# Copying negated scores to SBUF while their maximum is taken, in a planned attention-and-Fourier kernel

## The chip, the cores and the metric

The kernel runs on one core of a Trainium2 chip. Five engines work side by side, each through its own fixed list of instructions: TensorE (PE, with its weight loader PEld) multiplies matrices, VectorE (DVE), ScalarE (ACT) and GpSimd (POOL) work on tiles, and SyncE (SP) issues the transfers between HBM and SBUF. Engines wait for each other by semaphores. Matmuls write to PSUM, a small memory of banks of 512 float32 values per partition. The metric is the device time of one execution in microseconds. The kernel before takes 2978.28 us (median of 3 runs, 2978.08 to 2978.9).

## The reference

Two independent layers, their outputs side by side. All data are float32; S = 2048 rows, D = 1024 columns, 32 heads of 32 columns.

```python
qkv = x @ wqkv                       # 2048 x 1024 by 1024 x 3072, split in 32 heads
scores = q @ k.T * 32 ** -0.5        # per head: 2048 x 2048
p = softmax(scores, axis=-1)
a = (p @ v, heads joined) @ wo

re, im = xb @ dft_hid_re.T, xb @ dft_hid_im.T
b = dft_seq_re @ re - dft_seq_im @ im
out = concat([a, b], axis=-1)        # 2048 x 2048
```

The inputs of the attention half are scaled up by 8, so the scores spread widely and a softmax without its row maximum would overflow.

## The kernel before

**Dense products.** The products of the projections and of the Fourier layer are done by a seven-product scheme on 2 x 2 blocks (the products are numbered 1 to 7), and each product in three matmuls of a reduced-precision float type: every operand is split in a high part (a cast, line 475) and a low part (the difference, line 478), and high x high, low x high and high x low are summed in PSUM (line 389). Operands come by DMA, some after sums of two or three blocks (line 453), and results are combined out of PSUM by VectorE. In the planner these matmuls are the list `fills`, in one fixed order: the projections of x, then `dense1` and `dense2` of the Fourier layer, and last `project`, the output projection, whose operands need the result of attention.

**Attention, per head, twice over the scores.** `scores(h)` computes the 2048 x 2048 scores with queries on the partitions, in 32 tiles of 128 x 1024: two matmuls into a PSUM buffer of two banks (`psS`, two buffers, line 1193), a row maximum by VectorE, negated, into one column of `negm` (line 1199), and an exponential by ScalarE with that as its bias, which is wanted only for its row sum (`sums`, line 1202): the exponentials themselves are written back over the scores in PSUM and never read. From `negm` a per-row maximum is made, moved by DMA into two extra rows of the query operand, and `transposed(h)` then computes the same scores with keys on the partitions, maximum already subtracted, in 64 tiles of 128 x 512 (`psT`, two buffers, line 1316); ScalarE's exponential writes each into an SBUF tile `pt` or `ptl` (line 1320). Those tiles come from a ring of `NPT` = 27, five of them (`NLOW`) in another pool. After 5, 5 and 6 groups of four tiles (`ENDS`), a block of matmuls multiplies them with the values (line 1335) and gives the tiles back; VectorE adds the blocks up (lines 1346 and 1348).

**The order of work.** All engines' lists are written out ahead of time by a planner (`Plan`), a small simulation with a constant for each kind of operation (in us: `MAX` 1.22 for the row maximum, `ES` and `ET` for the two exponentials, `EVAC`, `CAST` and so on). A `Ring` stands for a set of buffers: `take()` gives the operations that must end before the next buffer is free. VectorE, ScalarE, GpSimd and SyncE take the ready operation of the lowest rank. TensorE chooses between three streams, S (score tiles), T (transposed tiles) and V (the blocks with the values), and the fills. An attention operation is taken only `LATE` = 0.25 us after its operands and buffers are free in the plan, as a reserve against the plan's errors. Scores may run ahead of the transposed tiles up to `LEAD`. A fill is taken when no stream is ready, or when the fills are behind their share of the work. The engines then keep the planned order at run time and wait where reality is later than the plan.

The first head's scores (h = 0) are computed while the first projection products still hold their buffers; heads 1 to 31 follow when the attention pools (`att()`, `att_low()`) have been opened.

Of the kernel before, what the change touches and what calls it, by code (L numbers as in the profile page):

```python
# [8 lines left out]
F32 = mybir.dt.float32  # L9
F32R = mybir.dt.float32r  # L10
AF = mybir.ActivationFunctionType
ALU = mybir.AluOpType
# [4 lines left out]
P = 128  # L17
S = 2048
# [3 lines left out]
NC = D // P  # L22
NS = S // P
NB = 512
NPT = 27
NE = 4
NLOW = 5
ENDS = (0, 5, 10, 16)
# [33 lines left out]
class Plan:  # L62
# [23 lines left out]
    def op(self, engine, cost, emit, after=(), uses=(), rank=0.0, kb=0, order=None, other=None, lanes=1, two=False):  # L86

        o = Op(engine, cost, emit, rank, kb, other, two)  # L90
        o.lanes = lanes
        seen = set()
        for d in after:
            if d is not None and id(d) not in seen:
                seen.add(id(d))
                self._wait(o, d)
        for u in uses:
            u.append(o)
        if order is not None:
            p, order.first = order.first, o  # L100
            if p is not None and not p.begun:
                p.soon.append(o)
                o.left += 1
        if o.left == 0:
            self._release(o)
        return o
# [104 lines left out]
def kernel(  # L211
# [11 lines left out]
    nc = tc.nc  # L223
# [26 lines left out]
    def f(ap):  # L250
        return ap.bitcast(F32)
# [74 lines left out]
    def att_low():  # L326

        att()
        return late["atl"]
# [6 lines left out]

    MM, PV, SWITCH, TINY = 0.2275, 0.853, 0.40, 0.17
    ES, ET = 1.235, 0.625
    MAX, EVAC, CAST, BIT = 1.22, 0.685, 0.415, 0.275
    SUB = 1.31  # L340
    ISSUE = 0.46

    LATE = 0.25
    HB = 0
    ACAST = 0.6
    RES = 400
# [11 lines left out]
    op = pl.op  # L358
# [798 lines left out]
    streams = {n: [] for n in "STV"}  # L1157
    psS_r, psT_r, pt_r, vt_r, rt_r, ot_r = Ring(2), Ring(2), Ring(NPT), Ring(2), Ring(1), Ring(2)
    small = {n: Ring(b) for n, b in (("st", 2), ("nm", 2), ("lh", 2), ("tw", 1))}
    qx_r = Ring(1)  # L1160
    got = {}
    Tops, Sops = {}, {}
    exp_of = {}
# [5 lines left out]
    def scores(h):  # L1169
        ST = {}  # L1170
        sold, suse = small["st"].take()
        maxes, exps = [], []
        if h:
            xold, xuse = qx_r.take()

            def load_x():
                att()
                g, r0 = divmod(h, 4)
                nc.sync.dma_start(f(QX[0])[0 : 3 * DH], qk_d[2 * g][0][r0 * DH : r0 * DH + DH].rearrange("d i c -> (d i) c"))

            got[h, "x"] = op("SP", ISSUE, load_x, [*xold, *qk_st[2 * (h // 4)][0], *(att_gate if h == 1 else [])], [xuse], -2, 192)
        for n, (qt, c) in enumerate([(k % 4, k // 4) for k in range(8)] + [divmod(k, 2) for k in range(8, 32)]):
            old, users = psS_r.take()
            own = h > 0 and qt < 4
            box = {}

            def mm(n=n, qt=qt, c=c, box=box, own=own):
                if n == 0:
                    ST["negm"] = sm.tile([P, 2, NS], F32, name="negm", bufs=2)
                    ST["sums"] = sm.tile([P, 2, NS], F32, name="sums", bufs=2)  # L1190
                box["p"] = p = psS.tile([P, 1024], F32, name="psS")
                for i in range(2):
                    nc.tensor.matmul(  # L1193
                        p[:, i * NB : i * NB + NB], (QX[0] if own else QS[h % 2])[:, qt * P : qt * P + P],
                        KS[h % 2][:, c * 1024 + i * NB : c * 1024 + i * NB + NB], start=True, stop=True,
                    )

            def mx(qt=qt, c=c, box=box):
                nc.vector.tensor_reduce(out=ST["negm"][:, c, qt : qt + 1], in_=box["p"], axis=AX.X, op=ALU.max, negate=True)  # L1199

            def ex(qt=qt, c=c, box=box):
                nc.scalar.activation(box["p"], box["p"], AF.Exp, bias=ST["negm"][:, c, qt : qt + 1], accum_out=ST["sums"][:, c, qt : qt + 1])  # L1202

            a = op("PE", 2 * MM, mm, [*old, *([got.get((h, "x"))] if own else [got.get((h, 0, qt // 4)), got.get((h, "z"))]), got.get((h, 1, 2 * c)), got.get((h, 1, 2 * c + 1))],
                   [users, xuse] if own else [users])
            b = op("DVE", MAX, mx, [a] + (sold if n == 0 else []), [users, suse], 0)
            e = op("ACT", ES, ex, [b], [users, suse], 0)
            exp_of[a] = e
            maxes.append(b)
            exps.append(e)  # L1210
            Sops.setdefault(h, []).append(a)
            streams["S"].append((a, h, n))
            if n == 5 and h:
                sums(h - 1)

        nold, nuse = small["nm"].take()
        lold, luse = small["lh"].take()
        box = {}

        def nmin():  # L1220
            ST["nm"] = sm.tile([P, NS], F32, name="nm", bufs=2)
            nc.vector.tensor_reduce(out=ST["nm"], in_=ST["negm"].rearrange("p c n -> p n c"), axis=AX.X, op=ALU.min)

        def high():
            box["l"] = sm.tile([P, 2, NS], F32R, name="lh", bufs=2)
            nc.vector.tensor_reduce(out=box["l"][:, 0], in_=ST["negm"].rearrange("p c n -> p n c"), axis=AX.X, op=ALU.min)

        def low():
            nc.vector.tensor_tensor(out=box["l"][:, 1], in0=ST["nm"], in1=f(box["l"])[:, 0], op=ALU.subtract)

        b = op("DVE", TINY, high, maxes + lold, [luse, suse], -2)
        a = op("DVE", TINY, nmin, maxes + nold, [nuse, suse], -2)
        c = op("DVE", TINY, low, [a, b], [nuse, luse], -2, two=True)
        def across():
            box["t"] = sm.tile([P, 2 * NS], F32, name="lt", bufs=2)
            nc.vector.transpose(box["t"], f(box["l"]).rearrange("p i s -> p (i s)"))

        d = op("DVE", TINY, across, [b, c], [luse], -2)

        put = op("SP", ISSUE, lambda: nc.sync.dma_start(m_d[h].rearrange("i (g p) -> g i p", g=4), box["t"]), [d], [luse], -3, 32)  # L1240
        moved = [op("SP", ISSUE, lambda: nc.sync.dma_start(f(QS[h % 2])[96:98, :], m_d[h].rearrange("(i q) p -> i (q p)", i=2)), [put], [], -3, 16)]
        mine[h] = (ST, suse, nuse, exps, moved)
# [59 lines left out]
    def transposed(h):  # L1302
# [4 lines left out]
        for t in range(NS):  # L1307
            for j in range(4):
                old, users = psT_r.take()
                here = pt_r.n % NPT < NLOW  # L1310
                pold, puse = pt_r.take()
# [6 lines left out]
                def ex(box=box, here=here):  # L1318
                    box["t"] = att_low().tile([P, NB], F32, name="ptl", bufs=NLOW) if here else att().tile([P, NB], F32, name="pt", bufs=NPT - NLOW)
                    nc.scalar.activation(box["t"], box["p"], AF.Exp)  # L1320
# [75 lines left out]
    while nf < len(fills) or any(place[n] < len(s) for n, s in streams.items()):  # L1396
# [18 lines left out]
        for n, (o, h, k) in heads.items():  # L1415
            if o.left:
                continue
            ready = o.ready + LATE
            if n == "V":
                ready = max(ready, room)  # L1420
            if ready > pl.now:
                times.append(ready)
                continue
            if n == "V":

                near = any(m in heads and heads[m][0].left == 0 and heads[m][0].ready + LATE < pl.now + NEAR and not (m == "S" and held) for m in "ST")
                if (near or stock < STOCK) and pl.now < o.ready + PATIENCE:
                    times.append(o.ready + PATIENCE)
                    continue
            rank = {"V": 0, "T": 1, "S": 0.5 if stock > SFIRST else 1.5}[n]  # L1430
            if n == "S" and "T" in heads and heads["T"][0].left == 0:
                th, tk = heads["T"][1:]
                lead = k / 33.0 * SST + 16 * (h - th - 1) - tk / 4
                if lead > LEAD:
                    continue
                if lead > 0:
                    rank = 2
            ok.append((rank, n))
        fill = None
        if nf < len(fills):  # L1440
            o, first, left = fills[nf]
            ready = o.ready if o.left == 0 else 1e18
            if first:
                ready = max(ready, room)
            if ready + (LATE if first else 0.0) <= pl.now:
                fill = o
            elif ready < 1e17:
                times.append(ready + LATE)
        if fill is not None and (not ok or (not first and left <= HB) or nf / (FILL - RES) <= done / ATT):
# [6 lines left out]
        if ok:  # L1456
            n = min(ok)[1]
            o = heads[n][0]
# [47 lines left out]
```

## Time and profile before

| What | Value |
|---|---|
| median of 3 runs | 2978.28 us (2978.08 to 2978.9) |
| profiled execution: span from its first to its last instruction | 2976.1 us |
| mean granted TensorE clock | 1.000 |
| busy: TensorE, weight loader | 99%, 72% |
| busy: VectorE, ScalarE, GpSimd | 81%, 77%, 29% |
| row maxima (line 1199) | 1024 of 1219 ns |
| exponentials of scores (line 1202), with a separate read of the sum | 1024 of 1143 ns, and 260 ns |
| exponentials of transposed tiles (line 1320) | 2048 of 654 ns |
| DMA | 58.6% of 16 engines' span, 188 GB/s |

Times are microseconds unless marked ns. An engine is busy while an instruction's record runs; records on one engine overlap a little, so a mean duration is longer than the distance from one start to the next. TensorE's matmuls are pipelined: one of 512 columns is on record for 390 ns, and the next starts long before that is over. The profile tells idle time before an instruction and what ended it ("<-").

### The profile page before, as it was taken

The numbers are of one execution on the slowest core, as the hardware profiler recorded it, in microseconds if no ns is written. First come the engines' busy times: TensorE is split into PE (matmuls) and PEld (weight loads), VectorE is DVE, ScalarE is ACT, GpSimd is POOL, SyncE is SP. The second block draws the span as 40 slices with busy tenths as digits, with TensorE's granted clock in tenths as the row PEclk, the third lists the DMA queues.
The fourth block names the chain that finished last, engine by engine and source line by source line (L and its number), as shares of the span: only waits on it lengthen the run. The fifth ranks groups of instructions, "written<-read, shape, count | busy, mean of one in ns | idle before, by whom it ended". The sixth has DMA issues, their size and how long they took to land. (4 is left out here: it accounts for less than half of the span.)

```text
span 2976.1 us, 45423 instructions
## 1 busy us (share of the span) xinstructions
PE 2950.9 (99%) x14912; PEld 2136.2 (72%) x14912; DVE 2403.6 (81%) x3237; ACT 2285.9 (77%) x4314; POOL 868.7 (29%) x641
## 2 busy tenths in 40 slices
PE   9999999999999999999999999999999999999999
PEld 7886766777777777777777667677777666677787
DVE  7678889788877877777778898888777888887696
ACT  5347888888888888888888888888888888887431
POOL 2312425122212332131102443332012534342152
PEclk9999999999999999999999999999999999999999
DMA  9974658666625655554425775555334775555662
GB/s 347 357 228 161 196 181 284 220 218 227 209 74 193 193 155 160 172 177 149 153 87 170 226 226 166 162 165 164 113 110 137 228 248 174 160 181 179 229 229 98
DMA packets 376576, 558.56 MB, mean 188 GB/s; under 512 B 111100, under 2 KB 111100, under 8 KB 376220
## 3 DMA queue, kind: packets, MB, share of 16 engines
q1 hardware_dynamic: 376344, 555.68, 58.6%
q8 instruction: 120, 1.97, 0.3%
q14 instruction: 112, 0.92, 0.1%
HBM read 402.42 MB, written 153.11 MB: 187 GB/s over the span
## 5 line engine op out<-in xcount | busy, mean ns | idle before, releaser
L1199 DVE TENSOR_REDUCE negm<-psS 128x1 f32<-128x1024 f32 x1024 | 1240.6, 1219 | 194.8 <-PE psS L1193 189.6
L1202 ACT ACTIVATE psS<-psS,negm 128x1024 f32<-128x1024 f32 x1024 | 1170.7, 1143 | 104.2 <-DVE negm L1199 99.2
L1320 ACT ACTIVATE pt<-psT 128x512 f32<-128x512 f32 x1668 | 964.9, 654 | 270.7 <-PE psT L1316 268.6
L389 PE MATMUL pd<-slot,h 128*128 128x512 f32 x3368 | 1145.7, 390 | 1.2 <-DVE ot L1346 0.9
L1316 PE MATMUL psT<-qs,ks 128*128 128x512 f32 x2048 | 804.9, 396 | 0.0
L389 PEld LDWEIGHTS pd<-slot,h 128*128 128x128 f32 x3368 | 632.3, 188 | 133.7 <-DVE h L475 1.3
L389 PE MATMUL pd<-slot,l 128*128 128x512 f32 x1684 | 656.4, 390 | 0.7 <-POOL l L478 0.7
L1316 PEld LDWEIGHTS psT<-qs,ks 128*128 128x128 f32 x2048 | 381.6, 188 | 169.5 <-issue 62.9
L1193 PE MATMUL psS<-ks,qs 128*128 128x512 f32 x1552 | 476.2, 392 | 7.1 <-ACT psS L1202 6.5
L478 POOL TENSOR_TENSOR l<-raw,h 128x512 fp32r<-128x512 f32 x160 | 214.6, 1341 | 828.9 <-PE psT L1316 344.8
L1335 PE MATMUL pd<-pt,vt 128*32 128x512 f32 x3336 | 430.6, 594 | 0.2
L453 POOL TENSOR_TENSOR raw<-raw,g 128x512 f32<-128x512 f32 x216 | 285.7, 1329 | 439.1 <-issue 74.8
L389 PEld LDWEIGHTS pd<-slot,l 128*128 128x128 f32 x1684 | 316.2, 188 | 67.4 <-POOL l L478 1.0
L1193 PEld LDWEIGHTS psS<-ks,qs 128*128 128x128 f32 x1552 | 288.5, 188 | 76.4 <-ACT psS L1202 17.9
L478 POOL TENSOR_TENSOR slot<-raw,slot 128x512 fp32r<-128x512 f32 x143 | 206.6, 1453 | 432.9 <-DVE slot L475 203.1
L1335 PEld LDWEIGHTS pd<-pt,vt 128*32 128x32 f32 x3336 | 111.3, 110 | 230.2 <-issue 216.4
L1320 ACT ACTIVATE ptl<-psT 128x512 f32<-128x512 f32 x380 | 224.5, 654 | 59.9 <-PE psT L1316 59.5
L1202 ACT ACTIVATION_READ_ACCUMULATOR psS<-psS,negm 128x1 f32 x1024 | 266.6, 260 | 0.0
L389 PE MATMUL pd<-slot,slot 128*128 128x512 f32 x768 | 193.4, 390 | 0.0
L389 PEld LDWEIGHTS pd<-slot,slot 128*128 128x128 f32 x768 | 144.2, 188 | 30.8
L475 DVE CAST h<-raw 128x512 fp32r<-128x512 f32 x321 | 148.8, 464 | 14.8 <-PE pd L389 10.7
L1348 DVE TENSOR_TENSOR ot<-ot,pd 128x512 f32<-128x512 f32 x64 | 44.0, 687 | 144.0 <-PE pd L1335 143.9
(121 smaller groups left out, 2254.6 us busy)
## 6 DMA issues: line engine op xcount, KB each, us to landing
raw<-in_ct SPq DMA_DIRECT2D x224, 256.0 KB
g<-in_ct SPq DMA_DIRECT2D x128, 256.0 KB
qk_d<-e SPq DMA_DIRECT2D x52, 512.0 KB
qs<-qk_d SPq DMA_DIRECT2D x128, 192.0 KB
ks<-qk_d SPq DMA_DIRECT2D x128, 192.0 KB
raw<-ab_d SPq DMA_DIRECT2D x96, 256.0 KB
c<-u_d SPq DMA_DIRECT2D x88, 256.0 KB
g<-ab_d SPq DMA_DIRECT2D x80, 256.0 KB
```

Of the source, the lines that this page charges most:

```text
L389: nc.tensor.matmul(box["ps"], a[1]((a[0].hi, a[0].lo)[u]()), b[1]((b[0].hi, b[0].lo)[v]()), start=k == 0, stop=k == n - 1)
L453: (nc.gpsimd if e == "POOL" else nc.vector).tensor_tensor(out=dest(), in0=dest() if a is None else a.get(), in1=other["q"] if "q" in other ...
L475: nc.vector.tensor_copy(hi(), raw())
L478: (nc.gpsimd if e == "POOL" else nc.vector).tensor_tensor(out=lo(), in0=raw(), in1=f(hi()), op=ALU.subtract)
L1193: nc.tensor.matmul(p[:, i * NB : i * NB + NB], (QX[0] if own else QS[h % 2])[:, qt * P : qt * P + P], KS[h % 2][:, c * 1024 + i * NB : c * ...
L1199: nc.vector.tensor_reduce(out=ST["negm"][:, c, qt : qt + 1], in_=box["p"], axis=AX.X, op=ALU.max, negate=True)
L1202: nc.scalar.activation(box["p"], box["p"], AF.Exp, bias=ST["negm"][:, c, qt : qt + 1], accum_out=ST["sums"][:, c, qt : qt + 1])
L1316: nc.tensor.matmul(box["p"], KS[h % 2][:, t * P : t * P + P], QS[h % 2][:, j * NB : j * NB + NB], start=True, stop=True)
L1320: nc.scalar.activation(box["t"], box["p"], AF.Exp)
L1335: nc.tensor.matmul(po["p"][j * DH : j * DH + DH, :], VT[h][:, k, :], box["t"], start=(k == t0), stop=(k == t), tile_position=(0, j * DH),)
L1348: nc.vector.tensor_tensor(out=po["o"], in0=po["o"], in1=po["p"], op=ALU.add)
```

## The change

For heads 1 to 31, VectorE no longer reduces the scores in PSUM; it multiplies them by -1 into an SBUF tile `srow` of 128 x 1024 (a ring of `NROW` = 2 rows in the lower attention pool) and accumulates their minimum on the way, which is the negated row maximum as before. ScalarE takes the exponential from that tile, with a scale of -1, and writes it back there. The PSUM buffer is then free after VectorE's pass; the SBUF row is free after the exponential. Head 0 is left as it was. The ring of exponential tiles shrinks from 27 to 24. In the planner the pass on VectorE costs `MOVE` = 1.25 in place of 1.22, and a score matmul is taken 1.2 us after its buffer is free in the plan (`SLATE`) in place of 0.25. Nothing else is edited; the planner works out all engines' orders anew.

```diff
-NPT = 27
+NPT = 24
+NROW = 2
...
+    MOVE = 1.25
...
-    LATE = 0.25
+    LATE, SLATE = 0.25, 1.2
...
+    row_r = Ring(NROW)
...
+            if h:
+                rold, ruse = row_r.take()
...
             def mx(qt=qt, c=c, box=box):
+                if h:
+                    box["s"] = att_low().tile([P, 1024], F32, name="srow", bufs=NROW)
+                    nc.vector.tensor_scalar(box["s"], box["p"], -1.0, None, op0=ALU.mult, op1=ALU.min, accum_out=ST["negm"][:, c, qt : qt + 1])
+                    return
                 nc.vector.tensor_reduce(out=ST["negm"][:, c, qt : qt + 1], in_=box["p"], axis=AX.X, op=ALU.max, negate=True)
 
             def ex(qt=qt, c=c, box=box):
+                if h:
+                    nc.scalar.activation(box["s"], box["s"], AF.Exp, scale=-1.0, bias=ST["negm"][:, c, qt : qt + 1], accum_out=ST["sums"][:, c, qt : qt + 1])
+                    return
                 nc.scalar.activation(box["p"], box["p"], AF.Exp, bias=ST["negm"][:, c, qt : qt + 1], accum_out=ST["sums"][:, c, qt : qt + 1])
...
-            b = op("DVE", MAX, mx, [a] + (sold if n == 0 else []), [users, suse], 0)
-            e = op("ACT", ES, ex, [b], [users, suse], 0)
+            b = op("DVE", MOVE if h else MAX, mx, [a] + (sold if n == 0 else []) + (rold if h else []), [users, suse, *([ruse] if h else [])], 0)
+            e = op("ACT", ES, ex, [b], [ruse if h else users, suse], 0)
...
-            ready = o.ready + LATE
+            ready = o.ready + (SLATE if n == "S" else LATE)
```

## The prediction

> **What bounds the kernel now.** I read the head of the page first, then the busy time by stage, then who waits for whom, then the matmuls one by one where they stall.
>
> ```profile
> span 2976.1 us, 45423 instructions
> PE 2950.9 (99%) x14912; PEld 2136.2 (72%) x14912; DVE 2403.6 (81%) x3237; ACT 2285.9 (77%) x4314; POOL 868.7 (29%) x641
> ```
>
> TensorE is busy in 99% of the span. The same question by stage (columns: stretch, its length, then busy us and instructions of each engine, granted clock, DMA share):
>
> ```profile
> 600.00:2600.00 2000.00, 1990.16 (x10283) 1412.46 (x10282) 1624.91 (x2178) 1694.72 (x3230) 564.55 (x423) 1.00 0.55 171
> 2717.00:2790.50 73.50, 73.50 (x411) 49.44 (x413) 39.01 (x71) 37.44 (x70) 1.67 (x1) 1.00 0.54 165
> 2790.50:2977.00 186.50, 181.56 (x805) 149.51 (x797) 154.28 (x197) 44.39 (x75) 72.01 (x46) 1.00 0.56 193
> ```
>
> Attention runs until 2790.5 us with dense matmuls between its own; what is left after it is dense alone. TensorE is full in every stretch, at clock 1.00. The change removes no matmul and adds none, so it can only win where TensorE waits, and it can lose anything. Which waits are there to win? (Columns: who waits, for whom, us in total, times, longest.)
>
> ```profile
> PEld psS L1193 <- ACT psS L1202: 30.7, 50, 1.7
> PE psS L1193 <- ACT psS L1202: 11.9, 21, 1.4
> ACT pt L1320 <- PE psT L1316: 268.6, 181, 6.7
> DVE negm L1199 <- PE psS L1193: 189.6, 350, 1.8
> ACT psS L1202 <- DVE negm L1199: 99.2, 136, 6.9
> ```
>
> The first two rows are the prize: score matmuls wait for the exponential that still holds their PSUM buffer. One such place in time order:
>
> ```profile
> 1298.18 0.69 DVE L453 TENSOR_TENSOR raw<-raw,g 128x512 f32<-128x512 f32 x1 [3.03 <-DMA raw<-in_xb]
> 1299.86 0.39 PE L389 MATMUL pd<-slot,l 128*128 128x512 f32 x1
> 1300.09 0.39 PE L389 MATMUL pd<-slot,h 128*128 128x512 f32 x1
> 1300.43 1.09 ACT L1202 ACTIVATE psS<-psS,negm 128x1024 f32<-128x1024 f32 x1 [1.73 <-DVE negm L1199]
> 1301.69 0.50 PE L1193 MATMUL psS<-ks,qs 128*128 128x512 f32 x1 [1.22 <-ACT psS L1202]
> ```
>
> Matmuls normally start 0.23 us apart (1299.86, 1300.09); here the next one comes 1.60 us later, so 1.37 us are lost. The first row is the root: VectorE, which works in a fixed order, stood 3.03 us before a late load, so the maximum, the exponential and the score matmul behind it were late in turn. The record of a matmul is 0.39 long, so a row's idle time understates a loss by 0.39 - 0.23 = 0.16. The 21 waits in TensorE's own row cost 11.9 + 21 x 0.16 = 15.3 us. The 50 in the weight loader's row that left the array no idle time cost at most 0.16 each, 8 us. **The prize is 15 to 23 us**; I take 18, since a wait too short to idle the array costs on average well under its bound. That is 0.6% of the time.
>
> **The change part by part.** It touches heads 1 to 31, so 31 x 32 = 992 score tiles. Rows that price VectorE's side:
>
> ```profile
> L1199 DVE TENSOR_REDUCE negm<-psS x1024: 1175/1219/1227, 71.9 to 2713.9; 128x1 f32<-128x1024 f32 x171
> L1264 DVE TENSOR_REDUCE rec<-tt 128x16 f32<-128x32 f32 x32 | 6.0, 188 | 1.1
> L745 DVE TENSOR_SCALAR slot<-pd x2: 681/682/683, 219.5 to 234.9; 128x512 f32<-128x512 f32 x2
> L1202 ACT ACTIVATION_READ_ACCUMULATOR psS<-psS,negm 128x1 f32 x1024 | 266.6, 260 | 0.0
> ```
>
> VectorE, removed: 992 reductions of 1.219 us. Added: 992 multiplications from PSUM to SBUF that also keep a minimum. From the two reductions an element costs (1219 - 188) / 992 = 1.04 ns; a multiplication of 512 elements takes 0.682, so one of 1024 takes 0.682 + 512 x 0.00104 = 1.215. That is the price of the reduction: writing the scores out is free in itself. What is not in the trace is VectorE's price for handing over the minimum. Lower end 0 (a gain is excluded, since the same elements pass at the same rate); upper end the 0.26 that ScalarE shows for reading its sum; nearest on the same engine is the 0.188 of a reduction of 32 elements, which like its neighbours overlaps the next instruction. I take 0.1, that is 992 x 0.1 = 99 us of VectorE time, 3.2 us per head. In the stretch 600 to 2600 it goes from 1625 to 1625 + 801 x 0.1 = 1705 us of 2000: still idle 15%, so not on TensorE's path by itself. If that cover were gone it would cost up to those 99 us. The plan charges 0.03 us more than before, so about 0.07 us per tile is lag that the plan does not know; VectorE sheds it at its idle moments before score tiles (350 of them, 189.6 us, above).
>
> [...]
>
> ScalarE's side:
>
> ```profile
> L1202 ACT ACTIVATE psS<-psS,negm 128x1024 f32<-128x1024 f32 x1024 | 1170.7, 1143 | 104.2 <-DVE negm L1199 99.2 <-DVE lh L1229 0.7 <-DVE tt L1263 0.7
> L473 ACT ACTIVATE slot<-er 128x512 fp32r<-128x512 f32 x52 | 32.4, 631 | 35.6 <-DVE er L453 13.1 <-PE psT L389 10.5 <-DMA er<-in_xa 6.0
> L741 ACT ACTIVATE acc<-psT 128x512 f32<-128x512 f32 x7 | 4.2, 600 | 8.3 <-PE psT L389 8.1
> L726 ACT ACTIVATE e<-psT 128x512 f32<-128x512 f32 x5 | 3.0, 591 | 3.7 <-PE psT L389 2.5 <-issue 1.2
> ```
>
> The exponential is the same, but reads and writes SBUF. The copies read SBUF at 0.631 and PSUM at 0.591 to 0.600, so I add 0.035 us x 992 = 35 us, 1.1 us per head (ends: 0 and 0.05, a little over the widest difference of these rows). The negated scale in the instruction costs nothing that I can see: same instruction, same operands. ScalarE has 2000 - 1695 = 305 us idle in 25 heads (a head takes 2000 / 25 = 80 us), 12 us per head, which covers it.
>
> [...]
>
> Buffers. A PSUM score buffer is now free after VectorE's pass; the exponential (1.143 and its accumulator) and its queue are off that path. In the plan the score matmul then waits 1.2 us beyond the release in place of 0.25. So a score matmul finds 0.95 us more reserve against lateness, and one engine fewer whose lateness it inherits. Of the 1.37 us shown, 0.42 would be left. Waits longer than 0.95 are few (the longest on record is 1.7). I put what is left at 3 us of the 18. **Gain: 15 us.**
>
> New waits. VectorE's pass now also waits for one of two SBUF rows, which the exponential of two tiles before frees, and the plan leaves no reserve there. Behind it on VectorE stand the evictions of the dense sums and the splitting of dense operands; TensorE waits for both, but they are made ahead:
>
> ```profile
> PE pd L389 <- DVE ot L1346: 0.9, 1, 0.9
> PE pd L389 <- DVE h L475: 0.2, 1, 0.2
> ```
>
> That is all that TensorE's own row shows of dense matmuls waiting for VectorE. I charge 2 us for this and the lag together, between 0 and 10.
>
> Three exponential tiles fewer (24 for 27). The last block of a head multiplies 6 x 4 = 24 tiles, so then the whole ring is held and no further transposed exponential can run until it is done. What ScalarE does in such a pause now:
>
> ```profile
> 1125.38 4.92 PE L1335 MATMUL pd<-pt,vt 128*32 128x512 f32 x42
> 1126.52 1.09 ACT L1202 ACTIVATE psS<-psS,negm 128x1024 f32<-128x1024 f32 x1 [0.86 <-DVE negm L1199]
> 1131.21 0.60 ACT L1320 ACTIVATE ptl<-psT 128x512 f32<-128x512 f32 x1 [3.48 <-PE psT L1316]
> ```
>
> It runs out of work anyway (3.48 us idle). The rows in SBUF let up to two more score tiles wait ready for it, 2 x 1.1 us; three transposed tiles less are 3 x 0.6. About even: I charge 0, because dense matmuls fill TensorE meanwhile. That cover ends: of the dense work, only what does not need attention's result can fill in.
>
> ```profile
> 2790.50:2977.00 186.50, 180.99 (x797) 149.51 (x797) 1.00 0.56 193
> ```
>
> This row is the dense matmuls alone after attention. The projection has 7 x 8 x 4 x 3 = 672, so some 125 x 0.23 = 29 us of other dense work are left. Attention may end 29 us later at no cost; beyond, each microsecond is lost. If it ends earlier nothing is won.
>
> No DMA, no SP or POOL instruction is added or moved; only the planned order around the waits shifts.
>
> **Sum** against the profiled span: 2976.1 - 15 + 2 = 2963. The median of the runs, 2978.28, lies 2.2 above that span, so 2965.
>
> **The rivals.** (1) *The wait only changes its name.* Score matmuls wait for VectorE, which is late through its longer passes and its waits for rows; the root shown above, a late load in front of VectorE, stays. For it: ScalarE's 99.2 us of waits for VectorE. Against: the 0.95 of reserve. The 18 come back nearly whole: 2977, within 0.2%.
>
> (2) *Attention is stretched past its cover*: slower. Place: ScalarE, at the pauses of the last block and in the dearer exponentials. Outside its pauses ScalarE idles little, so 1.1 us per head and 1 to 2 us for the missing tiles can add up to 2 us: 31 x 2 = 62, less 29 of cover, is 33 us lost: 2963 + 33 + 2 = 2998. It decides from 29 / 31 = 0.94 us per head on, and is slower than before from about 1.5. Against: the rows feed ScalarE in the same pauses.
>
> (3) *VectorE becomes the bound*: slower. At 0.26 for the hand-over it would be busy 1625 + 801 x 0.26 = 1833 of 2000. The plan then misses 0.23 x 32 = 7.4 us per head of the 15 that VectorE idles. If a quarter surfaces, 31 x 1.85 = 57 - 29 = 28 us, and the score waits come back: 2976 + 28 + 2 = 3006; with half, 3064.
>
> **How the numbers follow.** Forecast 0.55, its own range 2954 (all 23 us won, nothing charged) to 2972. Rival 1: 0.13. Rival 2: 0.20. Rival 3: 0.12. Faster 0.55, same 0.13, slower 0.32; 0.2% (6 us) is about what a measurement of this kernel tells from no change. The range 2953 to 3004 leaves out most of rival 3 and the far part of rival 2.
>
> **What would show it.** Right: the rows of score matmuls waiting for an exponential are gone and what takes their place is under 6 us; the pass on VectorE reads 1.21 to 1.23, with a hand-over near 0.1; the exponential reads 1.15 to 1.20; attention ends by 2790 at the latest. Rival 1: such waits for VectorE's pass of some 20 us. Rival 2: TensorE idle in the last 200 us, or attention ending after 2810. Rival 3: VectorE over 90% in the middle, with dense matmuls waiting for its casts and evictions. The prediction falls if attention's length, which I take as even, moves by more than 29 us upward.

## The result

The changed kernel takes 2988.5 us (median of 7 runs, 2985.86 to 2994.99) against 2978.9 us before (7 runs): ratio 1.0039, 95% interval 1.003 to 1.0049. It is slower by 0.4%; the forecast was 2965, 0.5% faster.

The head of the page of the changed kernel, and its busy time by stage (columns as in the prediction):

```profile
span 2988.7 us, 45652 instructions
PE 2957.1 (99%) x14912; PEld 2145.3 (72%) x14912; DVE 2395.0 (80%) x4180; ACT 2301.3 (77%) x4316; POOL 930.1 (31%) x688
240.00:600.00 360.00, 350.52 (x1745) 246.90 (x1744) 292.68 (x519) 292.26 (x550) 150.52 (x113) 0.98 0.66 211
600.00:2600.00 2000.00, 1990.81 (x10303) 1413.48 (x10302) 1623.23 (x2958) 1733.90 (x3281) 585.17 (x436) 1.00 0.54 169
```

TensorE does the same 14912 matmuls and is as full as before. In the long middle it even does 20 more in the same 2000 us, but of a mixture in which a matmul is not always the same work. In the first attention heads it falls behind outright: the same stretch before was

```profile
240.00:600.00 360.00, 355.03 (x1801) 246.23 (x1800) 305.88 (x413) 300.28 (x571) 123.18 (x89) 1.00 0.67 215
```

that is 1801 matmuls for 1745, and a granted clock of 1.00 for 0.98. What each group of the change costs now, and who waits for whom:

```profile
L1206 DVE TENSOR_SCALAR_CACHE_REDUCE srow<-psS 128x1024 f32<-128x1024 f32 x992 | 1203.1, 1220 | 211.2 <-ACT srow L1212 135.8 <-PE psS L1198 52.7 <-ACT pt L1332 11.6
L1206 DVE DVE_READ_ACCUMULATOR srow<-psS 128x1 f32 x992 | 81.3, 82 | 0.0
L1212 ACT ACTIVATE srow<-srow,negm 128x1024 f32<-128x1024 f32 x992 | 1197.1, 1214 | 15.1 <-DVE srow L1206 14.8
```
```profile
DVE srow L1206 <- ACT srow L1212: 135.8, 252, 1.2
PEld psT L1328 <- ACT srow L1212: 28.5, 34, 0.8
PEld psT L1328 <- issue: 25.2, 30, 0.8
PEld psT L1328 <- ACT pt L1332: 17.6, 50, 1.0
PEld psS L1198 <- DVE srow L1206: 6.5, 11, 2.1
PE pd L1347 <- DVE e L681: 3.5, 2, 2.8
PE psT L1328 <- ACT pt L1332: 3.5, 10, 0.6
PE psS L1198 <- DVE srow L1206: 2.9, 3, 1.7
PE psT L1328 <- DVE e L629: 2.0, 1, 2.0
PE pd L391 <- DVE ot L1358: 1.8, 1, 1.8
PE pd L391 <- DVE ot L1360: 1.4, 1, 1.4
```

The waits of score matmuls for their buffer are nearly gone (30.7 and 11.9 us before, 6.5 and 2.9 now). In their place stand waits of all other kinds of matmuls for VectorE and ScalarE, and VectorE itself waits 136 us for rows. Two rows before, for comparison:

```profile
PEld psT L1316 <- issue: 62.9, 75, 0.8
PEld psT L1316 <- ACT pt L1320: 9.7, 51, 0.3
```

The loader's 28.5 us behind the exponential of rows are not a new loss. These 34 waits are of 0.84 us each, as are the 30 put down to "issue" and the 75 before, and by matmul starts each costs the array 0.11 us. The 17.6 us behind the exponential of transposed tiles are new in part: the same number of waits, but up to 1.0 us long.

To add such things up I took every matmul's start from the trace and set its distance from the one before against the usual distance (0.227 us; 0.318 into and 0.523 out of a block with the values, and inside a block 0.007 within a group of four and 0.41 to 0.43 from group to group). The excess over it, in us, by stretch:

```
kernel                     span    excess  240-600  600-2600  2600-2810  after
before                     2976.1   48.0    14.5     31.4       0.9      -0.2
changed                    2988.7   60.1    22.6     31.6       3.9      -0.3
changed, planned anew      2983.9   54.7    18.5     30.1       4.5      -0.3
row reserve 0.4            2969.9   41.2    13.2     24.3       2.0       0.2
row reserve 0.4, anew      2965.9   37.9    14.3     20.3       1.6      -0.2
row reserve, heads 1 to 4  2971.2   42.8    15.7     23.0       2.2      -0.2
from head 4 on             2970.3   41.7    13.6     24.0       2.6      -0.2
```

The last five kernels are experiments that follow. The difference of the excesses before and after the change, 12.1 us, is that of the spans, 12.5. By kind, from 240 to 2810 us, a stall being an excess of more than 0.13 us: score matmuls, and all other matmuls by the engine whose work they waited for by the profile.

```
kernel                     score  other: VectorE  ScalarE  rest  half clock
before                      18.4        2.3          0.4    0.8     0.0
changed                      4.5       15.7          9.4    1.5     6.1
changed, planned anew        4.6       12.9          6.8    2.7     4.6
exponential charged          4.7       12.0          3.0    1.0     3.3
row reserve 0.4              1.5        8.3          7.7    1.1     0.0
row reserve 0.4, anew        0.8        5.9          6.2    1.1     1.7
row reserve 0.8              0.4        6.8          7.5    1.2     0.0
```

Score matmuls win 13.9 us; every other stall together goes from 3.5 to 26.5 (+23.0), and matmuls at half clock add 6.1. Differences under 0.13 us make up the rest (25.1 before, 20.9 now). By stretch, score stalls fall by 6.8 us in the first heads (240 to 600) and by 7.0 in the middle (600 to 2600), and other stalls grow by 10.3 and by 10.0. So the new stalls are as large in the middle as in the first heads, where the half clock comes on top.

The half clock is seen behind the stalls. TensorE and then VectorE in time order (columns: start, length, engine and line):

```profile
449.75 0.39 PE L1328 MATMUL psT<-qs,ks 128*128 128x512 f32 x1
451.93 0.50 PE L391 MATMUL pd<-slot,h 128*128 128x512 f32 x1 [1.79 <-DVE ot L1358]
452.27 0.40 PE L1328 MATMUL psT<-qs,ks 128*128 128x512 f32 x1
452.50 0.59 PE L391 MATMUL pd<-slot,l 128*128 128x512 f32 x1
452.89 1.05 PE L391 MATMUL pd<-slot,h 128*128 128x512 f32 x2
```
```profile
447.83 1.77 DVE L455 TENSOR_TENSOR raw<-raw,g 128x512 f32<-128x512 f32 x1
449.52 1.76 DVE L480 TENSOR_TENSOR l<-raw,h 128x512 fp32r<-128x512 f32 x1
451.20 0.68 DVE L1358 COPY ot<-pd 128x512 f32<-128x512 f32 x1
```

An addition and a difference of VectorE run beside the same kinds of operation on GpSimd and take 1.77 and 1.76 us; with none of those beside them, all 443 in this trace take 0.64 to 0.70, and of the 175 others the longest takes 1.80. The eviction behind them is late, TensorE idles 1.79 us, and from 452.5 on matmuls are 0.39 and more apart for 3.4 us, at a granted clock of 0.50.

### The profile page after: what moved, and what is told of

It reads as the page before. It is cut to its first block, busy times and chain, and to the rows that moved or that the text cites. A ratio compares the mean times of both kernels' runs of the same rounds, so it can differ in the third digit from the quotient of the medians.

```text
span 2988.7 us, 45652 instructions
## 1 busy us (share of the span) xinstructions
PE 2957.1 (99%) x14912; PEld 2145.3 (72%) x14912; DVE 2395.0 (80%) x4180; ACT 2301.3 (77%) x4316; POOL 930.1 (31%) x688
## 4 chain that ended last, share of the span: by engine, by line
PE 90%; DVE 3%; ACT 3%; DMA 1%; issue 1%; SPq 0%; POOL 0%; DVEq 0%; POOLq 0%
PE pd L391 40%; PE pd L1347 15%; PE psT L1328 15%; PE psS L1198 14%; PE psT L391 7%; ACT srow L1212 2%; ACT pt L1332 1%; DVE srow L1206 1%; DVE slot L477 1%; DMA c<-u_d 0%; ACT ptl L1332 0%; DMA raw<-in_wd 0%; DVE negm L1208 0%; DVE h L477 0%; DMA rt<-r_d 0%
## 5 line engine op out<-in xcount | busy, mean ns | idle before, releaser
L1206 DVE TENSOR_SCALAR_CACHE_REDUCE srow<-psS 128x1024 f32<-128x1024 f32 x992 | 1203.1, 1220 | 211.2 <-ACT srow L1212 135.8
L1212 ACT ACTIVATE srow<-srow,negm 128x1024 f32<-128x1024 f32 x992 | 1197.1, 1214 | 15.1 <-DVE srow L1206 14.8
L1332 ACT ACTIVATE pt<-psT 128x512 f32<-128x512 f32 x1618 | 924.3, 643 | 254.9 <-PE psT L1328 238.1
L391 PE MATMUL pd<-slot,h 128*128 128x512 f32 x3352 | 1111.4, 391 | 4.8 <-DVE ot L1358 1.8
L1328 PE MATMUL psT<-qs,ks 128*128 128x512 f32 x2048 | 752.5, 396 | 5.6 <-ACT pt L1332 3.5
L1328 PEld LDWEIGHTS psT<-qs,ks 128*128 128x128 f32 x2048 | 381.5, 188 | 157.5 <-ACT srow L1212 28.5
L480 POOL TENSOR_TENSOR l<-raw,h 128x512 fp32r<-128x512 f32 x167 | 226.1, 1355 | 796.0 <-DVE h L477 576.9
L1347 PE MATMUL pd<-pt,vt 128*32 128x512 f32 x3236 | 396.6, 597 | 1.6 <-DVE slot L896 1.1
L1332 ACT ACTIVATE ptl<-psT 128x512 f32<-128x512 f32 x430 | 249.0, 639 | 109.7 <-PE psT L1328 102.8
L1212 ACT ACTIVATION_READ_ACCUMULATOR srow<-srow,negm 128x1 f32 x992 | 257.7, 260 | 0.0
L1347 PE MATMUL pd<-ptl,vt 128*32 128x512 f32 x860 | 165.9, 600 | 4.2 <-DVE e L681 3.5
```

The costliest lines, as they stand in the source:

```text
L391: nc.tensor.matmul(box["ps"], a[1]((a[0].hi, a[0].lo)[u]()), b[1]((b[0].hi, b[0].lo)[v]()), start=k == 0, stop=k == n - 1)
L480: (nc.gpsimd if e == "POOL" else nc.vector).tensor_tensor(out=lo(), in0=raw(), in1=f(hi()), op=ALU.subtract)
L1206: nc.vector.tensor_scalar(box["s"], box["p"], -1.0, None, op0=ALU.mult, op1=ALU.min, accum_out=ST["negm"][:, c, qt : qt + 1])
L1212: nc.scalar.activation(box["s"], box["s"], AF.Exp, scale=-1.0, bias=ST["negm"][:, c, qt : qt + 1], accum_out=ST["sums"][:, c, qt : qt + 1])
L1328: nc.tensor.matmul(box["p"], KS[h % 2][:, t * P : t * P + P], QS[h % 2][:, j * NB : j * NB + NB], start=True, stop=True)
L1347: nc.tensor.matmul(po["p"][j * DH : j * DH + DH, :], VT[h][:, k, :], box["t"], start=(k == t0), stop=(k == t), tile_position=(0, j * DH),)
```

## The experiments

All ratios are to the kernel before on the same chip, with a 95% interval. Four theories are named in the expectations: A, ScalarE's dearer exponential and the waits for rows; B, fewer tiles; C, any new order meets new accidents; D, the longer reserve. E came later: the loss is in the first heads.

**Another order of the kernel before.** What does a new plan alone do?

```diff
-    MAX, EVAC, CAST, BIT = 1.22, 0.685, 0.415, 0.275
+    MAX, EVAC, CAST, BIT = 1.25, 0.685, 0.415, 0.275
```

> The kernel before with one planner constant changed: the row maximum is charged at 1.25 us in place of 1.22, so all orders are worked out anew and nothing that is computed changes. Theory A (the exponential out of SBUF is dearer than the plan knows, 1.13 us from start to start for 1.09, so ScalarE and behind it VectorE run late): no loss here, 2979 within 0.2%. Theory B (24 exponential tiles for 27 cost the time): the same, 2979. Theory C (any new order meets new accidents, such as a late load in front of VectorE, and a matmul engine that stands for 1.8 us or more goes on at half clock): this moves too, by 4 to 10 us either way.

Measured 2974.19 us, ratio 0.9994 (0.9985 to 1.0003). C as the whole cause falls, as far as one new order tells: it moves this kernel by 0.06%.

**24 tiles alone.**

```diff
-NPT = 27
+NPT = 24
```

> The kernel before with 24 exponential tiles in place of 27 and nothing else. Theory B: slower by 8 us or more, attention ends later than 2800. Theory A: within 0.2% of 2979, since ScalarE idles in the pauses anyway. Theory C: 4 to 10 us either way.

Measured 2977.32, ratio 1.0001 (0.9992 to 1.001). B falls.

**VectorE's pass alone**, with the exponential still in PSUM; nothing reads the rows.

```diff
-                    nc.scalar.activation(box["s"], box["s"], AF.Exp, scale=-1.0, bias=ST["negm"][:, c, qt : qt + 1], accum_out=ST["sums"][:, c, qt : qt + 1])
+                    nc.scalar.activation(box["p"], box["p"], AF.Exp, bias=ST["negm"][:, c, qt : qt + 1], accum_out=ST["sums"][:, c, qt : qt + 1])
...
-            b = op("DVE", MOVE if h else MAX, mx, [a] + (sold if n == 0 else []) + (rold if h else []), [users, suse, *([ruse] if h else [])], 0)
-            e = op("ACT", ES, ex, [b], [ruse if h else users, suse], 0)
+            b = op("DVE", MOVE if h else MAX, mx, [a] + (sold if n == 0 else []) + [], [users, suse, *([ruse] if h else [])], 0)
+            e = op("ACT", ES, ex, [b], [users, suse], 0)
...
-    LATE, SLATE = 0.25, 1.2
+    LATE, SLATE = 0.25, 0.25
```

The buffer is released by the exponential again, and the plan has no wait for rows.

> VectorE's pass alone: it writes the negated scores to SBUF and accumulates the minimum, but nobody reads them; the exponential stays in PSUM on the held buffer, the reserve is 0.25, 24 tiles, no waits for rows. Theories A and D: the pass takes what the maximum took (1.149 to the next start for 1.135), so 2974 to 2982, the kernel before again, with its 19 us of score matmuls waiting for the exponential. If the pass itself is what hurts (its accumulator read, its writes beside GpSimd's): 2986 or more.

Measured 2976.57, ratio 0.9997 (0.9988 to 1.0006). Its groups:

```profile
L1206 DVE TENSOR_SCALAR_CACHE_REDUCE srow<-psS 128x1024 f32<-128x1024 f32 x992 | 1203.0, 1220 | 197.0 <-PE psS L1198 191.3
L1212 ACT ACTIVATE psS<-psS,negm 128x1024 f32<-128x1024 f32 x992 | 1141.1, 1150 | 69.2 <-DVE srow L1206 63.3 <-DVE tt L1275 1.5 <-DVE lh L1241 0.9
```

The copy to SBUF, the 24 tiles and the accumulator read are free within 0.12%, and by matmul starts stalls other than those of score matmuls stay at 4.1 us (3.5 before). VectorE waits for no row here. The exponential reads 1.150 in PSUM; in the changed kernel, from SBUF, 1.214.

**The longer reserve alone**, on the kernel before.

```diff
-    LATE = 0.25
+    LATE, SLATE = 0.25, 1.2
...
-            ready = o.ready + LATE
+            ready = o.ready + (SLATE if n == "S" else LATE)
```

> The kernel before with the longer reserve alone: a score matmul is taken 1.2 us after its PSUM buffer is free in the plan; maximum and exponential stay in PSUM, 27 tiles. Score matmuls lost 19 us to waits for the exponential before. Theories A and B: those waits shrink to under 6 us and nothing else is made worse, so 2964 to 2972, unless two PSUM buffers held 0.95 us longer stretch attention: its end, 2790 us, then moves beyond 2815 and the time is over 2979. Theory C: anything from 2965 to 2990.

Measured 3295.18, ratio 1.1072 (1.1057 to 1.1087). The expectation had named this way out, attention ending beyond 2815, but no size near this one:

```profile
600.00:2560.00 1960.00, 1935.41 (x9786) 1396.05 (x9785) 1581.29 (x2187) 1481.71 (x2763) 562.85 (x411) 1.00 0.57 182
2560.00:3120.00 560.00, 446.95 (x1708) 208.76 (x1706) 253.42 (x273) 442.13 (x821) 1.26 (x2) 0.79 0.09 25
```

With the buffer held through the exponential and 0.95 us more, attention runs slower (it ends at 3120 in place of 2791). The dense matmuls fill in until about 2560 and are then used up, DMA falls to 0.09, GpSimd stops, and TensorE stands between attention's own matmuls at a granted clock of 0.79. It is rival 2 of the prediction, with the price that it can have; in the changed kernel, where the buffer is freed earlier, the same reserve does not do this: attention ends at 2793.

**The changed kernel without the longer reserve.**

```diff
-    LATE, SLATE = 0.25, 1.2
+    LATE, SLATE = 0.25, 0.25
```

> The changed kernel with the reserve of score matmuls back at 0.25 us. The replanned kernel before stayed within 0.1%, and so did 24 tiles alone, so neither is the cause. Theory A (ScalarE's dearer exponential and VectorE's waits for rows, which the plan leaves without reserve): score matmuls now wait for VectorE's pass as they did for the exponential, 10 to 20 us of stalls on top of those of the changed kernel: 2990 to 3005. Theory D (the longer reserve itself costs, since it stretches attention as it does alone, 3295 us): attention ends earlier than 2793 and the time falls to 2980 or less.

Measured 3005.65, ratio 1.0095 (1.0081 to 1.0109).

```profile
PEld psS L1198 <- DVE srow L1206: 24.2, 38, 2.1
PE psS L1198 <- DVE srow L1206: 10.9, 21, 1.7
```

Without it the score matmuls wait for VectorE as they had waited for ScalarE. It comes out just above what A had. The reserve is needed, and it is not what costs in the changed kernel. D falls.

**The exponential charged at what it takes.**

```diff
-            e = op("ACT", ES, ex, [b], [ruse if h else users, suse], 0)
+            e = op("ACT", 1.265 if h else ES, ex, [b], [ruse if h else users, suse], 0)
```

> The changed kernel with the exponential of heads 1 to 31 charged at 1.265 us in the plan in place of 1.235, which is what it takes (1.042 to its accumulator read, 0.091 on to the next start, and the 0.13 by which the plan lets instructions overlap). Theory A: VectorE's 136 us of waits for rows fall by half or more, the new stalls of TensorE with them, and the time comes down from 2988 to 2975 or less. Theory B: stays at 2985 to 2990. Theory C: 4 to 10 us either way, with the row waits falling or not.

Measured 2984.81, ratio 1.0024 (1.0014 to 1.0034). About a third of what A promised, and VectorE's waits for rows fell only from 136 to 110 us. Up to 2810 us, though, the excess fell from 60.4 to 46.5, under the 48.3 of the kernel before; the stalls behind ScalarE went from 9.4 to 3.0, those behind VectorE from 15.7 to 12.0. Against it stands a new loss at the end:

```profile
2845.26 1.22 PE L391 MATMUL psT<-slot,slot 128*128 128x512 f32 x2 [3.88 <-DVE slot L480]
```

Attention ends 8 us later (2801), and fewer dense matmuls besides the projection's 672 are left behind it (76, in the changed kernel 172). So the projection starts at 2818 us in place of 2832, and some of its operands are not ready when their turn comes: 3.88 us idle, and 6.8 us at half clock behind it (mean granted clock of this run 0.997).

**Both middling: the charge and a reserve of 0.6.**

```diff
-    LATE, SLATE = 0.25, 1.2
+    LATE, SLATE = 0.25, 0.6
...
+            e = op("ACT", 1.265 if h else ES, ex, [b], [ruse if h else users, suse], 0)
```

> The changed kernel with the exponential charged at 1.265 us and the reserve of score matmuls at 0.6 us. Theory A: the stalls of the charged kernel (24 us) and attention's end near 2790 again in place of 2801, so that the projection starts without a gap: 2972 to 2980. Theory D: as A, 2980 or less, through the earlier end alone. If neither: 2985 as with the charge alone.

Measured 2983.57, ratio 1.0021 (1.0013 to 1.003). The end is at 2793 again without a gap, but score matmuls wait for VectorE (25.3 us in the loader's row). The expectation failed: what was gained at the one place was lost at the other.

**A reserve on the rows.** The plan lets VectorE use a row only some time after the exponential that frees it.

```diff
-        return d.end + (self.LAT_PE if e == "PE" else self.LAT) + self.SLACK.get((e, o.engine), 0.0)
+        return d.end + (self.LAT_PE if e == "PE" else self.LAT) + self.SLACK.get((e, o.engine), 0.0) + (d.late if o.engine == "DVE" else 0.0)
...
             exp_of[a] = e
+            e.late = 0.4 if h else 0.0
```

> The changed kernel, but the plan lets VectorE take a row only 0.4 us after the exponential that frees it has ended in the plan (the same holds for VectorE's other waits for these exponentials). Theory A: the 136 us that VectorE waits for rows fall under 60, the dense work behind it comes in time, TensorE's new stalls shrink by half, 2975 to 2982, unless attention's end moves later than 2800. Theory D: attention stretched further, 2990 or more.

Measured 2973.3, ratio 0.9989 (0.998 to 0.9998): 15 us less than the changed kernel and just under the one before.

```profile
DVE srow L1207 <- ACT srow L1213: 75.3, 148, 1.2
```

The waits for rows fall to 75 us, no half clock shows during the work (mean granted clock 1.000), attention ends at 2784. The time came out 2 us better than expected, and TensorE's new stalls shrank by half as expected (other stalls and half clock from 32.6 to 17.1 us); the waits for rows missed the 60 us. Most of it is the half clock (6.1 us) and the stalls behind VectorE (15.7 to 8.3). With 17.1 us of other stalls, the kernel is still far from the 3.5 before.

**The size of that reserve**: 0.2 and 0.8 in place of 0.4.

> As the row reserve of 0.4 us, with 0.2. Theory A (VectorE's waits for rows, which the plan leaves without reserve, cost the time): between none (2988, ratio 1.0039) and 0.4 (ratio 0.9989), so 2976 to 2985, and VectorE's waits for rows between 136 and 75 us. Theory C (a lucky order): no such order between the three.

> As the row reserve of 0.4 us, with 0.8. Theory A: the waits for rows fall further, under 50 us, and the time stays at 2970 to 2977, or rises only if attention then ends later than 2795. Theory C: anything up to 2990, with the waits for rows falling all the same.

Measured 2976.68, ratio 1.0001 (0.9992 to 1.001), and 2982.8, ratio 1.0019 (1.001 to 1.0028). With 0.8 the waits for rows are nearly gone:

```profile
DVE srow L1207 <- ACT srow L1213: 13.5, 33, 0.9
```

and the time is worse again, for the reason seen above: attention ends at 2799, the projection starts at 2812 and then waits for its operands (stalls of 2.72 and 3.61 us and 6.8 us of half clock, 10 us of excess after 2810; mean granted clock of this run 0.999). With 0.2 the waits for rows hardly fall (124 us), yet the time comes back by 12 us. So the total of these waits is not the measure of the loss.

**The changed kernel, planned anew.**

```diff
-    MOVE = 1.25
+    MOVE = 1.22
```

> The changed kernel with VectorE's pass charged at 1.22 us in place of 1.25: a new order and nothing else, as a measure of the scatter of plans of this kind. Theory A: still slow, 2982 to 2995, with 110 to 160 us of waits for rows. Theory C: as likely to be below 2980 as above.

Measured 2985.5, ratio 1.0032 (1.002 to 1.0044). Slow again, as A had it: the loss is no matter of one unlucky order.

**Row reserve 0.4 with a score reserve of 0.8.**

```diff
-    LATE, SLATE = 0.25, 1.2
+    LATE, SLATE = 0.25, 0.8
```

> The row reserve of 0.4 us with the reserve of score matmuls at 0.8 in place of 1.2. The reserve of 0.6 left 18 us of score matmuls waiting for VectorE, 1.2 left 5. Theory A: with VectorE less late, 8 to 12 us of such waits, so 2972 to 2980; a gain over 2973 only if attention's earlier end counted, which it does not while TensorE is full.

Measured 2980.95, ratio 1.0014 (1.0005 to 1.0023). A little above what was expected, and 8 us worse than with 1.2. Score matmuls lose 9.6 us, as expected, where they lost 1.5.

**The change from head 4 on only.** Heads 0 to 3 stay as they were, reserve included.

```diff
-            if h:
-                rold, ruse = row_r.take()
+            if h > 3:
+                rold, ruse = row_r.take()
...
-            ready = o.ready + (SLATE if n == "S" else LATE)
+            ready = o.ready + (SLATE if n == "S" and h > 3 else LATE)
```

> The changed kernel with the change from head 4 on only; heads 0 to 3 stay in PSUM with the old reserve of 0.25 us. Theory E (the loss is in the first heads, 240 to 600 us, where transfers are densest and stalls reach the half clock): 2976 to 2981, with that stretch losing 15 us as before. Theory A in its first form (waits for rows everywhere): 2984 to 2989, since 28 of 31 heads still wait for rows, 100 to 130 us.

Measured 2972.92, ratio 0.9986 (0.9978 to 0.9995).

```profile
240.00:600.00 360.00, 355.77 (x1805) 248.55 (x1804) 306.75 (x461) 303.88 (x576) 129.84 (x94) 1.00 0.67 213
DVE srow L1206 <- ACT srow L1212: 114.7, 221, 0.9
```

1805 matmuls in the early stretch, as before the change (1801). The same edit without its first heads is a small gain. But E explains only half of it: against the changed kernel the excess falls by 9.0 us in the first heads and by 7.6 in the middle, where the change and most of its waits for rows stand as they were (115 us in all). Nor are those harmless: other stalls in the middle are 8.2 us, and 2.8 before.

**A row reserve in heads 1 to 4 only.**

```diff
-            e.late = 0.4 if h else 0.0
+            e.late = 0.4 if 0 < h < 5 else 0.0
```

> The changed kernel with the row reserve of 0.4 us in heads 1 to 4 only. Theory E: most of the gain, 2974 to 2981, with 13 to 16 us lost in 240 to 600. Theory A: little of it, 2983 to 2989, the waits for rows still above 110 us.

Measured 2975.69, ratio 0.9991 (0.9982 to 1.0), with 135.4 us of waits for rows. The same from the other side, and again only in part: the excess falls by 6.9 us in the first heads and by 8.6 in the middle, which has no reserve.

**Row reserve 0.4, planned anew** (`MOVE` 1.22).

> The row reserve of 0.4 us in all heads with VectorE's pass charged at 1.22 in place of 1.25: another order of the same plan. Theories A and E: 2971 to 2979 again. A lucky order: above 2982.

Measured 2969.11, ratio 0.9973 (0.9962 to 0.9984): the best of all, 8 us under the kernel before. The gain of the row reserve is not one lucky order. Three kernels have now been planned anew, and their ratios moved by 0.0006, 0.0007 and 0.0016. So much two orders of one kernel can differ, and smaller differences between experiments tell nothing.

## Why the prediction was wrong

**Right.** *The prize and its price.* 15 to 23 us of score waits were put down, 18 taken, 3 said to be left: 18.4 and 4.5 by matmul starts. *VectorE's pass*: 1.215 said, 1.220 measured. *24 tiles*: charged at nothing, measured at nothing. *Attention's length*: taken as even, its end moved from 2791 to 2793 (3 us past the 2790 that the prediction gave as a sign of being right).

**Right in kind, wrong in size.** VectorE's handing over of the minimum was priced at 0.1 us. The trace has it as 992 accumulator reads, instructions of their own, with 0.082 on record; but a pass takes only 1.149 from its start to the start of the next instruction, against 1.135 for the reduction, so the price is 0.014. The exponential was priced at 0.035 more and takes 0.064 more on record (1.150 in PSUM with the same pass in front, 1.214 from SBUF), and 0.045 more from its start to that of its accumulator read (0.997 and 1.042).

**The step that failed: "New waits ... I charge 2 us for this and the lag together, between 0 and 10."** The place was named (VectorE's pass waits for a row without reserve, and evictions and operands stand behind it), and waved through because TensorE's rows before showed only 0.9 and 0.2 us of waits for VectorE. But those rows showed a plan in which VectorE's one long instruction never waited for ScalarE. In the changed kernel stalls other than those of score matmuls went from 3.5 to 26.5 us by matmul starts, 23 in place of 2. That alone outweighs the 14 won. On top came 6.1 us at half clock, which the prediction did not have at all.

Two waits are in these 23 us. 13.4 are behind VectorE; at the same score reserve of 1.2 us, a row reserve of 0.4 took off half of them or more and most of the half clock, in two orders each (second table above). 9.0 are transposed matmuls behind ScalarE. The prediction had ScalarE's dearer exponential covered by 12 us of idle time per head, but the plan did not know of it: in the two kernels that charge it in the plan these stalls are 3.0 and 3.6 us, in the others with rows from head 1 on 5.9 to 12.2.

The row reserve brought back 15 us of time where the change had lost 10. The charge brought back 13.9 us of excess up to 2810 us and lost 8 behind it. So it is shown that the loss comes from a plan that counts on rows and exponentials earlier than they come. How much of it is the missing reserve and how much the exponential that is charged too low is not separated, since the two were not run together.

**Where.** The excess grew by 8.1 us in the first heads, half clock included, and by 0.2 in the middle. But the forecast was a fall, and in the middle the new stalls used up what the score matmuls had won there. The two runs that spare the first heads are as fast as the kernel before or a little faster, and half of what they win back lies in the middle. In the first heads transfers are densest (DMA share 0.66 against 0.54 in the middle), and VectorE is late for other reasons too, as in the lines at 447 to 452 us; that this is why the half clock comes there is argued, not shown.

**The rivals.** Rival 1 (*the wait only changes its name*) is nearest, but with the wrong matmuls at the end of it: score matmuls hardly wait for VectorE, dense ones do, and transposed ones wait for ScalarE. Rival 2 did not happen in the changed kernel, and it did in three experiments; its point of decision, 29 us of dense work left behind attention, was put too high, since ends of 2799 and 2801, only 8 to 10 us later, already led to stalls. By then 56 and 76 dense matmuls besides the projection's were left, 13 and 17 us of work; it sufficed up to the projection's start, but not until all of the projection's operands were ready. Rival 3 is excluded: VectorE is busy 1623 us of the 2000 in the middle, 1625 before.

**What stays open.** In the middle stretch the excess is 31.6 us in the changed kernel and 23.0 with the reserve in heads 1 to 4 only, at 136 and 135 us of waits for rows; why that order runs better there too was not traced. How much of the stalls behind VectorE is the row wait and how much collisions of VectorE with GpSimd was not separated. With the row reserve 13 to 17 us of other stalls are left where 3.5 were before, so the change keeps less than the forecast gain even then. A third row, which would take most of the wait itself away, wasn't tried.

## What to carry to other kernels

In an order fixed ahead, a buffer moved from one wait to another needs its reserve moved too: here the same edit was 0.4% slower with none on the new wait and 0.1 to 0.3% faster with 0.4 us, and too much of it (0.8) cost again at the end, where the projection then waited for its operands. When an in-order engine gets a new thing to wait for, price everything queued behind it, and do not take its harmlessness from a trace in which it never waited. Look for the loss by stretch and by kind: in a kernel full to 99%, a stretch whose total has not changed can hide a gain that new stalls have used up.

## What the runs showed of the hardware

Stalls of TensorE of about 2 us can be followed by half clock, and need not be. In the changed kernel an idle time of 1.99 us is:

```profile
264.16 0.73 PE L1328 MATMUL psT<-qs,ks 128*128 128x512 f32 x2 [1.99 <-DVE e L629]
264.73 0.99 PE L1198 MATMUL psS<-ks,qx 128*128 128x512 f32 x2
265.52 0.63 PE L1328 MATMUL psT<-qs,ks 128*128 128x512 f32 x1
265.95 0.63 PE L391 MATMUL pd<-slot,l 128*128 128x512 f32 x1
```

and with the row reserve one of 1.98 at the same place is not:

```profile
263.50 0.74 PE L1330 MATMUL psT<-qs,ks 128*128 128x512 f32 x2 [1.98 <-DVE e L630]
265.04 0.40 PE L392 MATMUL pd<-slot,l 128*128 128x512 f32 x1
265.27 0.62 PE L392 MATMUL pd<-slot,h 128*128 128x512 f32 x2
265.73 0.39 PE L392 MATMUL pd<-slot,l 128*128 128x512 f32 x1
```

In the first, matmuls are 0.43 apart from 265.52 on, at a granted clock of 0.50 from 264.79 to 268.20 us; in the second they are 0.23 apart, and the mean granted clock of the whole run is 1.000. What made the difference between the two is not shown.

In the changed kernel, before the end of the work, the trace's record of the clock turns to half at 264.79, 452.53 and 503.73 us, for 3.41, 3.41 and 6.83 us. So by estimate, at half the work in these stretches, one such stall cost 1.7 to 3.4 us beside its own length. The turns are 187.73 and 51.20 us apart, which is 55 and 15 times the 3.413 us of the two shorter stretches.

From 80 us on, TensorE has five idle times of over 1.40 us in the changed kernel. Those of 1.79 and 1.99 us were followed by half clock; in that of 2.80 us the clock turned after 1.91. Those of 1.41 and 1.73 us were not followed by it, nor was the longest in the kernel before, of 1.40. The "1.8 us or more" of an expectation fits these, but not the 1.98 us with the row reserve. So the length of a stall alone does not tell, and it is no rule.
